# Fourteen matmuls of zeros ahead of TensorE's first inputs, in a two-layer FNet/H3 kernel

## The chip, the cores and the metric

One core of one Trainium2 chip. The metric is the device time of one execution in microseconds (us). TensorE is called PE in the profile, its weight loads PEld, VectorE DVE, ScalarE ACT, GpSimd POOL, and SyncE, which issues most loads, SP.

## The reference

Two layer kinds alternate, A B A B, each with a layer norm ahead of it and a residual around it; S = 2048 rows, D = 576 columns, f32.

```python
a = einsum("bsd,ed->bse", x, dft_hid_re); b = einsum("bsd,ed->bse", x, dft_hid_im)
A(x) = einsum("ts,bse->bte", dft_seq_re, a) - einsum("ts,bse->bte", dft_seq_im, b)
B(q, k, v): k_shift = causal conv of k with 4 taps;  kv = k_shift * v
            y = irfft(rfft(kv padded) * rfft(ssm_k padded)) + kv * ssm_D;  q * y
x = x + A(ln(x)); x = x + B(ln(x), k, v); x = x + A(ln(x)); x = x + B(ln(x), k, v)
```

## The kernel before, in words

The first A layer is turned round: the sequence transform comes first and the hidden one after it. `layer` (L300) runs steps (tb, g, k): for each block tb of 512 output rows and each of two matrices g (real and imaginary), 16 steps k multiply the normalised rows X[k] (128 rows of x) with the tile of the matrix that is loaded for that step. Every f32 operand is split into a rounded high part (ACT, `split`, L98) and the rest as a low part (DVE, L99), and a product is three matmuls: high x high, high x low, low x high. So a step is 14 matmuls of 512 columns: three into each of the accumulators s0 to s3 and two into rm. The order inside a step in the program is s0, s0, s0, s1, ..., rm, rm.

What a step needs:

- the matrix tile c: a 256 KB load by SP (L168; the first one L216), its high part by ACT (L98, `mats<-flts`), its low part by DVE (L99). Three tiles (`cs`) are kept, so the split of tile n+3 waits for the last matmul of step n.
- the row tile X[k]: a load (L683), statistics on DVE (L181 to L183), a power on POOL (L184), the bias on DVE (L190), the scaling on ACT (L191), then the high part on ACT (L195, `mats<-early`) and the low part on DVE (L197, L198). Rows from 8 on take their sums on ACT instead (L649, L651), with L650 and L652 on DVE, the power on POOL (L653), L675 on DVE and L676 on ACT.

Beside these steps runs `branch` (from L349): the convolution of k on DVE (L393 products, L398 sums, 128x1152 elements a piece) and the first stage of the long convolution, `f1_products` (L441): six matmuls of 288 or 384 columns into two of three banks bf0 to bf2, which ACT then copies out (L451) and stores (L452). It takes its data from loads of v and ssm_k (L418), split by L98 and L99 into `f1r`.

The start of the main program (L746 to L768) issues the pieces by hand: the branch's first loads, row 0, the first two c tiles, the first two groups of f1_products, row 1. Which instruction stands behind which on each engine is then settled by a scheduling layer under the kernel: it lists the instructions of each engine by its own estimate of when each could run, within the dependences that it finds and the edges that `issue_after` adds. On the chip every engine runs its list in order. All matmuls are recorded at one helper line, L75, so they are told apart here by their tiles: `s`, `rm`, `bf`, and later `bk`.

Of the kernel before, what the change touches and what calls it, by code (L numbers as in the profile page):

```python
# [10 lines left out]
F32 = mybir.dt.float32  # L11
# [4 lines left out]
P = 128  # L16
# [3 lines left out]
J = S // P  # L20
TB = 4
NT = 512
# [3 lines left out]
EPS = 1e-5  # L26
ASTAT = 8
XLEAD = 3
EARLY = 6
ROWS = (0, 1, 2, 3, 4, 5, 6, 7, 8, 9)  # L30
K_FIRST = 4
# [34 lines left out]
def fnet_h3_kernel(ctx: ExitStack, tc: tile.TileContext, x, c_mat, w_re, w_im, k_pad, v, shift_k,  # L66
                   ssm_k, ssm_d, f1c, i2c, midc, out):
    nc = tc.nc
# [5 lines left out]
    def mm(ps, lhsT, rhs, first, last, more=False):  # L74
        return nc.tensor.matmul(ps, lhsT, rhs, start=first, stop=last, skip_group_check=more).ins  # L75
# [10 lines left out]
    acc4 = [psp.tile([P, NT], F32, tag=f"s{i}", name=f"s{i}") for i in range(4)]  # L86
# [44 lines left out]
    def lay(t, at, *sizes):  # L131

        for name, words, n in sizes:
            ring.setdefault(name, Ring()).tiles.extend(t[:, at + i * words:at + (i + 1) * words] for i in range(n))
            at += n * words
        assert at <= t.shape[1], (at, t.shape, sizes)
        return at
# [9 lines left out]
    xs = mats[:, :X_END].rearrange("p (j n) -> p j n", j=J)  # L147
# [18 lines left out]
    def load_after(dst, src):  # L166
        with tc.issue_after(anchor[-1]):
            return nc.sync.dma_start(dst, src).ins  # L168
# [44 lines left out]
    def load_c(step):  # L213
        g, tb, k = step
        raw = ring["craw"]()
        anchor.append(load_after(raw, c_mat[g, tb, k]) if anchor else nc.sync.dma_start(raw, c_mat[g, tb, k]).ins)  # L216
        c = ring["cs"]()
        t = c[:, :NT], c[:, NT:]
        with behind(*stored):
            halved[:] = split(t[0], t[1], raw)  # L220
        CT[step] = t
# [3 lines left out]
    def load_w():  # L225
        lay(flts, SC_AT + CRAW * NT + 4 * D, ("wl", D, 3))
        wg = region_a(FR, "w").rearrange("p (k n) -> p k n", k=9)
        for ch in (8, *range(8)):
            w = two(wg[:, ch])
            raw = ring["wl"]()  # L230
            if ch < 8:
                nc.sync.dma_start(raw, (w_re if ch < 4 else w_im)[(ch % 4) * P:(ch % 4 + 1) * P, :])
            else:
                nc.sync.dma_start(raw[:REM], w_re[NC * P:, :])
                nc.sync.dma_start(raw[REM:], w_im[NC * P:, :])
            for lo, hi, sg in ((0, P, 1 if ch < 4 else -1),) if ch < 8 else ((0, REM, 1), (REM, P, -1)):
                if sg > 0:
                    split(w[lo:hi, 0, :], w[lo:hi, 1, :], raw[lo:hi])
                else:
                    nc.scalar.activation(w[lo:hi, 0, :], raw[lo:hi], AF.Copy, scale=-1.0)  # L240
                    nc.vector.scalar_tensor_tensor(w[lo:hi, 1, :], raw[lo:hi], -1.0,  # L241
                                                   w[lo:hi, 0, :].bitcast(F32), op0=OP.mult,
                                                   op1=OP.subtract)
            W[ch] = w
            yield
        for ch in range(9):
            load_after(w_d[ch], wg[:, ch].bitcast(F32))
            yield
# [42 lines left out]
    def finish(pending, pieces):  # L291
        while pending and pieces:
            if not isinstance(pending[0], types.GeneratorType):
                pending[0] = hidden(*pending[0])
            if next(pending[0], 0) == 0:
                pending.pop(0)
            else:
                pieces -= 1

    def layer(get_x, xres, done, pending, blocks=TB):  # L300
        steps = [(g, tb, k) for tb in range(blocks) for g in range(2) for k in range(J)]
        for n, (g, tb, k) in enumerate(steps):
# [3 lines left out]
            if n + 2 < len(steps):  # L306
                load_c(steps[n + 2])
            for i in range(XLEAD + 1 if blocks == TB else 1):
                if n + i < J:
# [346 lines left out]
    def gated(xa, q, j, junk=None, last=None):  # L656
        load_after(q, yb_d[j])
        if junk is None:
            mv, rs, _ = norm_stats(xa)
            mean, op = mv[:, 0:1], OP.subtract  # L660
        else:
            mean, rs, _ = sums(xa, junk)
            op = OP.add
        yield
        nc.vector.scalar_tensor_tensor(q, xa, mean, q, op0=op, op1=OP.mult)
        for i in range(2 if last else 1):
            cs = slice(i * HD, (i + 1) * HD) if last else slice(None)
            nc.vector.scalar_tensor_tensor(q[:, cs], q[:, cs], rs, xa[:, cs], op0=OP.mult, op1=OP.add)
            if last:
                last(i, cs)  # L670
# [9 lines left out]
    def load_x(j):  # L680
        if j < J:
            XL[j] = ring["x"]()
            nc.sync.dma_start(XL[j], x[:, j, :])  # L683
# [7 lines left out]
    def get_x0(j):  # L691
        if X[j] is None:
            if j > 0:
                load_x(j + 2)
            stats0(j)
            if j > 0:
                with behind(*stored):
                    stats0(j + 1)
            src, ln = LN[j]
            with behind(*rounded[-1:]):  # L700
                next(ln, 0)
            X[j] = to_x(src, j)
# [4 lines left out]
    def make_x1(j):  # L707
        xa, q = ring["xa"](), ring["yb"]()
        load_after(xa, xa_d[j])
        for _ in gated(xa, q, j, ring["xj"]() if j % 2 and j >= EARLY else None):  # L710
            yield
# [9 lines left out]
    def advance(j=None):  # L721
        while to_store:
            load_after(*to_store.pop(0))
        with behind(*halved, *added, *evac):
            for row in list(making):
                if next(row, 0) == 0:
                    making.remove(row)
            if j is not None:
                making.append(make_x1(j))
                next(making[-1])  # L730
# [4 lines left out]
    def done1(j, xa):  # L735
# [7 lines left out]
        if j < J - 1:  # L743
            nc.sync.dma_start(out[:, j, :], q)

    pending = []  # L746
    lay(flts, SC_AT, ("craw", NT, CRAW))
    br = branch()
    wl = load_w()
    load_x(0)  # L750
    next(br)
    get_x0(0)
    with tc.issue_after(biased[0]):
# [18 lines left out]
    for n, whole in layer(get_x0, lambda j: x[:, j, :], done0, pending):  # L772
# [40 lines left out]
        if 0 <= m and n < HOLD:  # L813
            advance(m // 2 if m % 2 == 0 and m < 2 * EARLY else None)
    T, R, t7 = {}, {}, []
# [195 lines left out]
    for n, whole in layer(get_x1, lambda j: xb_d[j], done1, pending, 1):  # L1011
# [4 lines left out]
        if n == 0:  # L1016
            for name, at in (("xa", 0), ("yb", 4 * D)):
# [3 lines left out]
                lay(gate, at, (name, D, 4))  # L1021
        advance(EARLY + ROWS.index(n) if n in ROWS else None)
        finish(pending, 1)
# [131 lines left out]
```

## Time and profile before

| | us |
|---|---|
| median of 3 runs | 1190.23 |
| lowest and highest of them | 1188.69, 1192.36 |
| the profiled execution's own time | 1191.32 |
| its span, first to last instruction | 1189.5 |
| PE busy in the span | 1168.5 (98%) |
| DVE, ACT busy | 872.8 (73%), 650.0 (55%) |

The profiled execution took 1191.32 us, of which 1.82 us lie outside the span. Times in the views are counted from the span's start. A timeline row is: start, duration, engine, line, operation, output<-input, shapes, count, and in brackets the idle time of the engine before it with what ended that. Rows of one kind that follow each other without a gap are merged, so a row "x10" holds ten instructions. PE's matmuls overlap in the records (one lasts about 0.4 us, the next starts 0.23 us behind it), so the pace of PE is read from starts, not from durations.

### The profile page before, as it was taken

The numbers are of one execution on the slowest core, as the hardware profiler recorded it, in microseconds if no ns is written. First come the engines' busy times: TensorE is split into PE (matmuls) and PEld (weight loads), VectorE is DVE, ScalarE is ACT, GpSimd is POOL, SyncE is SP. The second block draws the span as 40 slices with busy tenths as digits, with TensorE's granted clock in tenths as the row PEclk, the third lists the DMA queues.
The fourth block names the chain that finished last, engine by engine and source line by source line (L and its number), as shares of the span: only waits on it lengthen the run. The fifth ranks groups of instructions, "written<-read, shape, count | busy, mean of one in ns | idle before, by whom it ended". The sixth has DMA issues, their size and how long they took to land.

```text
span 1189.5 us, 18071 instructions
## 1 busy us (share of the span) xinstructions
PE 1168.5 (98%) x6184; PEld 987.2 (83%) x6184; DVE 872.8 (73%) x1562; ACT 650.0 (55%) x1279; POOL 75.1 (6%) x116
## 2 busy tenths in 40 slices
PE   7999999999999999999999999999999999999997
PEld 5776767888888888888888898888888888889997
DVE  7899983688777778787767665865776776775764
ACT  7865555567766668766645666534444445450200
POOL 2210000000000000001101111000000000001111
PEclk9999999999999999999999999999999999999999
DMA  9869898545656656648966777772772776795621
GB/s 340 295 197 306 269 290 267 178 139 177 225 189 198 200 160 204 186 137 239 273 197 226 235 246 231 251 250 73 255 248 71 240 273 248 266 322 158 214 83 41
DMA packets 147454, 255.65 MB, mean 215 GB/s; under 512 B 16161, under 2 KB 56353, under 8 KB 147362
## 3 DMA queue, kind: packets, MB, share of 16 engines
q1 hardware_dynamic: 111890, 210.17, 54.9%
q10 hardware_dynamic: 28560, 37.91, 9.1%
q0 software_dynamic: 6912, 6.43, 2.4%
q8 instruction: 48, 0.79, 0.3%
q14 instruction: 44, 0.36, 0.1%
HBM read 187.80 MB, written 66.65 MB: 214 GB/s over the span
## 4 chain that ended last, share of the span: by engine, by line
PE 76%; ACT 2%; DVE 2%; DMA 2%; issue 1%; POOLq 0%; ACTq 0%; DVEq 0%
PE s L75 42%; PE bk L75 29%; PE rm L75 4%; ACT flts L512 1%; ACT mid L512 1%; DMA t<-ud 1%; DVE mid L518 0%; DMA yb<-flts 0%; DMA flts<-vd 0%; DMA flts<-in_c_mat 0%; DVE flts L532 0%; DVE flts L530 0%; ACT u L98 0%; DVE flts L531 0%; DVE flts L533 0%
## 5 line engine op out<-in xcount | busy, mean ns | idle before, releaser
L75 PE MATMUL s<-mats 128*128 128x512 f32 x2088 | 543.0, 395 | 1.6 <-ACT mats L195 0.8
L75 PEld LDWEIGHTS s<-mats 128*128 128x128 f32 x2088 | 381.0, 188 | 83.2 <-issue 10.6
L99 DVE TENSOR_TENSOR mats<-flts,mats 128x512 fp32r<-128x512 f32 x206 | 141.0, 688 | 50.8 <-ACT mats L98 48.4
L98 ACT ACTIVATE mats<-flts 128x512 fp32r<-128x512 f32 x206 | 128.3, 628 | 82.6 <-PE bk L75 31.2
L75 PE MATMUL bk<-mid 128*128 128x288 f32 x704 | 127.7, 302 | 1.6 <-DVE flts L287 0.8
L75 PEld LDWEIGHTS bk<-mid 128*128 128x128 f32 x704 | 108.0, 188 | 23.7 <-ACT flts L512 5.8
L512 ACT ACTIVATE flts<-bk 128x288 f32<-128x288 f32 (+1 forms) x192 | 76.3, 406 | 90.8 <-PE bk L75 75.9
L75 PE MATMUL bk<-w,u 128*128 128x288 f32 x864 | 121.3, 296 | 1.0 <-DVE w L241 0.4
L75 PEld LDWEIGHTS bk<-w,u 128*128 128x128 f32 x864 | 117.3, 188 | 5.5 <-DVE flts L532 1.7
L518 DVE TENSOR_TENSOR mid<-flts,mid 128x576 fp32r<-128x576 f32 (+1 forms) x149 | 93.4, 629 | 18.6 <-ACT mid L512 15.2
L75 PE MATMUL rm<-mats 128*128 128x512 f32 x304 | 94.6, 391 | 0.2 <-ACT flts L512 0.2
L512 ACT ACTIVATE mid<-flts 128x576 fp32r<-128x576 f32 (+1 forms) x148 | 80.3, 575 | 11.8 <-DVE flts L533 8.5
L287 DVE TENSOR_TENSOR flts<-flts,bk 128x288 f32<-128x288 f32 x48 | 21.8, 453 | 65.8 <-PE bk L75 65.7
L451 ACT ACTIVATE flts<-bf 128x384 f32<-128x384 f32 (+1 forms) x104 | 43.2, 463 | 46.0 <-PE bf L75 45.9
L75 PE MATMUL bk<-mats 128*128 128x288 f32 (+1 forms) x376 | 67.8, 317 | 0.0
L75 PEld LDWEIGHTS rm<-mats 128*128 128x128 f32 x304 | 56.9, 188 | 12.8 <-ACT flts L512 0.6
L75 PE MATMUL s<-t,mats 128*128 128x512 f32 x264 | 65.4, 390 | 0.6 <-DVE t L99 0.3
L184 POOL TENSOR_TENSOR flts<-flts 128x1 f32<-128x1 f32 x35 | 28.7, 821 | 522.4 <-DVE flts L183 522.3
L75 PE MATMUL bk<-mats,t 128*128 128x288 f32 (+1 forms) x368 | 59.3, 303 | 0.0
L512 ACT ACTIVATE flts<-flts 64x288 f32<-64x288 f32 x128 | 56.6, 443 | 4.7
L75 PEld LDWEIGHTS s<-t,mats 128*128 128x128 f32 x264 | 49.4, 188 | 11.7 <-DVE t L99 0.8
L75 PEld LDWEIGHTS bk<-mats 128*128 128x128 f32 x376 | 55.5, 188 | 3.4
(146 smaller groups left out, 1496.7 us busy)
## 6 DMA issues: line engine op xcount, KB each, us to landing
flts<-in_c_mat SPq DMA_DIRECT2D x148, 256.0 KB, 3.3
ph<-in_c_mat SPq DMA_DIRECT2D x54, 512.0 KB, 4.5
flts<-in_c_mat SPq DMA_DIRECT2D x30, 512.0 KB, 4.8
flts<-td SPq DMA_DIRECT2D x53, 288.0 KB, 2.9
td<-flts ACTq DMA_DIRECT2D x36, 384.0 KB, 4.6
vd<-flts ACTq DMA_DIRECT2D x64, 144.0 KB, 2.7
flts<-vd SPq DMA_DIRECT2D x32, 288.0 KB, 4.1
ud<-ph ACTq DMA_DIRECT2D x12, 512.0 KB, 6.3
```

The costliest lines, as they stand in the source:

```text
L75: return nc.tensor.matmul(ps, lhsT, rhs, start=first, stop=last, skip_group_check=more).ins
L98: a = nc.scalar.activation(h, src, AF.Copy).ins
L99: return a, nc.vector.tensor_tensor(l, src, h.bitcast(F32), OP.subtract).ins
L184: pows.append(nc.gpsimd.tensor_tensor(rs, ve, mhalf, OP.pow).ins)
L287: added[:] = [nc.vector.tensor_tensor(r[:, cs], r[:, cs], ps[:, :HD], OP.add).ins]
L451: stored[:] = [nc.scalar.activation(so[:, i, :], ps[i], AF.Copy).ins]
L512: last_act.append(nc.scalar.activation(*args, **kw).ins)
L518: nc.vector.tensor_tensor(l, src, h.bitcast(F32), OP.subtract)
```

## The change

A constant and a helper are added, and the helper is called between the first row's load and the first f1_products.

```diff
+WARM = 14
...
+    def warm():
+        t = xs[:, J - 1, :NT]
+        nc.vector.memset(t.bitcast(F32), 0.0)
+        for i in range(WARM):
+            mm(acc4[3], t[:, :P], t, i == 0, i == WARM - 1)
+
     pending = []
     lay(flts, SC_AT, ("craw", NT, CRAW))
     br = branch()
     wl = load_w()
     load_x(0)
+    warm()
     next(br)
     get_x0(0)
```

`xs[:, J - 1, :NT]` is the place where row tile 15 will be written, 15 steps later; `acc4[3]` is the accumulator s3, which step 0 starts afresh. One memset on DVE is added, 128 partitions x 512, and 14 matmuls 128x128 by 128x512 on PE. No load and no store is added or taken out.

The scheduling layer sorts the lists anew, though. All orders differ only in the first part of the program: PE's last difference stands at the 471st of its 6186 matmuls, DVE's at the 216th of 1564 instructions, ACT's at the 186th, SP's at the 66th. POOL's list is the same. Line numbers of the changed kernel are higher by one here, because of the new constant (L75 is L76, L195 is L196).

At the start of PE's list, before the change, with bf the banks of f1_products and s0, s1 the first accumulators of step 0:

```order
L75 MATMUL bf1_67<-f1r_151 128x288
L75 MATMUL bf0_66<-f1r_151 128x288
L75 MATMUL s0_69<-mats_73 128x512 x2
L75 MATMUL bf0_66<-f1r_151 128x288
L75 MATMUL bf2_68<-f1r_151 128x288
...
L75 MATMUL s0_69<-mats_73 128x512
L75 MATMUL s1_70<-mats_73 128x512 x3
```

And with it:

```order
L76 MATMUL s3_72<-mats_73 128x512 x14
L76 MATMUL bf1_67<-f1r_166 128x288
L76 MATMUL bf0_66<-f1r_166 128x288
...
L76 MATMUL s0_69<-mats_73 128x512
L76 MATMUL s1_70<-mats_73 128x512
L76 MATMUL s0_69<-mats_73 128x512
L76 MATMUL s1_70<-mats_73 128x512
L76 MATMUL bf0_66<-f1r_166 128x288
L76 MATMUL bf2_68<-f1r_166 128x288
...
L76 MATMUL s0_69<-mats_73 128x512
L76 MATMUL s1_70<-mats_73 128x512
```

The zeros stand first, and two matmuls of step 0 into s1 have moved ahead of the second group of f1_products.

On ACT the same stretch, from the split of c tile 1 to the high part of row 1 (L195), before:

```order
L98 ACTIVATE mats_73<-flts_75 128x512
L451 ACTIVATE flts_75<-bf1_67 128x288
L451 ACTIVATE flts_75<-bf0_66 128x288
L98 ACTIVATE f1r_151<-flts_75 128x576
L452 DMA td_78<-flts_75 256x1x288
L451 ACTIVATE flts_75<-bf2_68 128x288
L451 ACTIVATE flts_75<-bf0_66 128x288
L98 ACTIVATE f1r_151<-flts_75 128x576
L191 ACTIVATE early_74<-early_74,flts_75 128x576
L98 ACTIVATE mats_73<-flts_75 128x512
L195 ACTIVATE mats_73<-early_74 128x576
```

And with the change:

```order
L99 ACTIVATE mats_73<-flts_75 128x512
L452 ACTIVATE flts_75<-bf0_66 128x288
L452 ACTIVATE flts_75<-bf1_67 128x288
L99 ACTIVATE f1r_166<-flts_75 128x576
L453 DMA td_78<-flts_75 256x1x288
L452 ACTIVATE flts_75<-bf2_68 128x288
L452 ACTIVATE flts_75<-bf0_66 128x288
L192 ACTIVATE early_74<-early_74,flts_75 128x576
L99 ACTIVATE f1r_166<-flts_75 128x576
L196 ACTIVATE mats_73<-early_74 128x576
L99 ACTIVATE mats_73<-flts_75 128x512
```

Bank bf0, which the second group needs back, is copied out first; the scaling and the high part of row 1 stand ahead of the split of c tile 2.

On DVE, from behind the bias of row 1 to the low part of row 1 (L198), before:

```order
L183 TENSOR_SCALAR flts_75<-flts_75 128x1
L181 BN_STATS flts_75<-early_74 128x6 x2
L99 TENSOR_TENSOR f1r_151<-flts_75,f1r_151 128x576
L182 BN_AGGR flts_75<-flts_75 128x2
L190 TENSOR_SCALAR flts_75<-flts_75 128x1
L183 TENSOR_SCALAR flts_75<-flts_75 128x1
L181 BN_STATS flts_75<-early_74 128x6 x2
L190 TENSOR_SCALAR flts_75<-flts_75 128x1
L182 BN_AGGR flts_75<-flts_75 128x2
L181 BN_STATS flts_75<-early_74 128x6
L197 TENSOR_TENSOR mats_73<-early_74,mats_73 128x64
L198 TENSOR_TENSOR mats_73<-early_74,mats_73 128x512
```

And with the change:

```order
L184 TENSOR_SCALAR flts_75<-flts_75 128x1
L182 BN_STATS flts_75<-early_74 128x6 x2
L191 TENSOR_SCALAR flts_75<-flts_75 128x1
L183 BN_AGGR flts_75<-flts_75 128x2
L182 BN_STATS flts_75<-early_74 128x6
L184 TENSOR_SCALAR flts_75<-flts_75 128x1
L182 BN_STATS flts_75<-early_74 128x6
L100 TENSOR_TENSOR f1r_166<-flts_75,f1r_166 128x576
L198 TENSOR_TENSOR mats_73<-early_74,mats_73 128x64
L199 TENSOR_TENSOR mats_73<-early_74,mats_73 128x512
```

Three instructions of later rows' statistics (one BN_STATS, one BN_AGGR, one bias) that stood ahead of row 1's low part now stand behind it.

## The prediction

> **What bounds the kernel now.** I read the page first, then the list of PE's waits, then PE's timeline of the first 19 us, then the engines that feed it. From the page, PE's line (busy time, share of the span, instructions), and from the waits the three longest (total, times, longest):
>
> ```profile
> PE 1168.5 (98%) x6184; PEld 987.2 (83%) x6184; DVE 872.8 (73%) x1562; ACT 650.0 (55%) x1279; POOL 75.1 (6%) x116
> ```
>
> ```profile
> PE bf L75 <- DVE f1r L99: 6.6, 1, 6.6
> PE bf L75 <- ACT flts L451: 1.7, 3, 1.2
> PE s L75 <- ACT mats L195: 0.8, 1, 0.8
> ```
>
> PE is busy for 98% of the span, and most of what is missing is the first wait: 6.6 us until f1_products has its operands. So PE's own pace sets the time, and what brings its work forward counts, unless a later wait eats it. PE's timeline shows that the pace is not the same everywhere:
>
> ```profile
> 6.58 1.09 PE L75 MATMUL bf<-f1r 64*128 64x288 f32 x6 [6.58 <-DVE f1r L99]
> 7.82 0.79 PE L75 MATMUL s<-mats 128*128 128x512 f32 x1
> 8.92 0.80 PE L75 MATMUL s<-mats 128*128 128x512 f32 x1 [0.30 <-DVE mats L99]
> 9.94 1.09 PE L75 MATMUL bf<-f1r 64*128 64x288 f32 x6 [0.22 <-ACT flts L451]
> 10.95 4.46 PE L75 MATMUL s<-mats 128*128 128x512 f32 x10
> 15.26 0.63 PE L75 MATMUL rm<-mats 128*128 128x512 f32 x2
> 15.73 2.90 PE L75 MATMUL s<-mats 128*128 128x512 f32 x12
> 18.47 0.61 PE L75 MATMUL rm<-mats 128*128 128x512 f32 x2
> ```
>
> Ten matmuls start between 10.95 and 15.26, 0.431 us apart; the twelve from 15.73 to 18.47 are 0.228 apart. The same form, 128x512, runs at about half pace up to 15.2 us and at full pace behind that. (The page's clock line shows full clock from the first slice on; for the start the starts of the matmuls are the evidence.) Full pace came 5.3 us after 9.94, where PE's work first runs on without a gap; the short bursts from 6.58, with gaps of 0.15, 0.30 and 0.22 us, had not brought it.
>
> **The change, part by part.** *The memset* is one more DVE instruction, behind the first of these rows of DVE's timeline:
>
> ```profile
> 0.81 0.06 DVE L174 MEMSET flts<- 128x1 f32 x1 [0.81 <-PEq L1147]
> 3.64 0.82 DVE L181 BATCH_NORM_STATS2 flts<-early 128x6 f32<-128x288 f32 x2 [2.77 <-DMA early<-in_x]
> ...
> 8.92 0.69 DVE L198 TENSOR_TENSOR mats<-early,mats 128x512 fp32r<-128x512 f32 x1
> ```
>
> A memset of 128x512 isn't in the trace. Its bounds are 0.06 us (the 128x1 memset) and 0.69 (a two-input operation of its size); I take 0.6, nearer to the row of its size. It lies in DVE's idle 2.77 us, in which DVE waits for the first row, so it costs nothing; without that cover it would cost its 0.6.
>
> *The zeros* start at about 0.87 + 0.6 = 1.5 us. At half pace fourteen take 14 x 0.431 = 6.0 us and end at 7.5; at full pace 14 x 0.228 = 3.2, ending at 4.7. PE's real work waits until 6.58, so they overrun it by 0.9 us at most. Queued behind them is the first group of f1_products, and for that waits ACT's copy L451:
>
> ```profile
> 9.19 0.69 ACT L451 ACTIVATE flts<-bf 128x288 f32<-128x288 f32 x2
> ...
> 11.67 0.68 ACT L98 ACTIVATE f1r<-flts 128x576 fp32r<-128x576 f32 x1
> 12.24 0.86 ACT L191 ACTIVATE early<-early,flts 128x576 f32<-128x576 f32 x1
> 13.03 0.63 ACT L98 ACTIVATE mats<-flts 128x512 fp32r<-128x512 f32 x1
> 13.57 0.67 ACT L195 ACTIVATE mats<-early 128x576 fp32r<-128x576 f32 x1
> ```
>
> The copies start only at 9.19, because the split of c tile 1 stands ahead of them on ACT. A first group that starts at 7.5 and takes the 1.09 of its row ends at 8.6: hidden. And the zeros' 6.0 us without a gap are longer than the 5.3 that brought full pace in the trace, so I take it that full pace is there when real work comes, or within a few matmuls.
>
> The Trainium skill, "TensorE: Matmul & The Clock Gate", section "Part 1: The HAM clock gate", puts the two paces down to a clock at half rate until a window of about 3.4 us was busy, with windows that don't start with the kernel. The trace's 0.431 against 0.228 agrees with the halving. By that rule a run of 6.0 us can just miss a whole window, since one is sure only in 6.8 us; then full pace would come later, which is the third rival.
>
> *Step 0.* The second group waits for a copy, and bf0 is now copied first: 9.19 plus half of 0.69 is about 9.6 instead of 9.94. At full pace the group takes about half of 1.09, 0.6 us. Two matmuls into s1 now stand before it, in waits that are there anyway. Ten are left, 10 x 0.228 = 2.3 us: PE is through with step 0 at 9.6 + 0.6 + 2.3 = 12.5, against 15.73. These 3.2 us are the most that the pace can give.
>
> *Step 1 is late next.* It needs row 1, whose bias (the first of these DVE rows) and low part (the last) are
>
> ```profile
> 11.82 0.21 DVE L190 TENSOR_SCALAR flts<-flts 128x1 f32<-128x1 f32 x1 [0.35 <-POOL flts L184]
> ...
> 14.46 0.21 DVE L190 TENSOR_SCALAR flts<-flts 128x1 f32<-128x1 f32 x1
> 14.59 0.20 DVE L182 BATCH_NORM_AGGREGATE flts<-flts 128x2 f32<-128x12 f32 x1
> 14.71 0.41 DVE L181 BATCH_NORM_STATS2 flts<-early 128x6 f32<-128x288 f32 x1
> 15.03 0.21 DVE L197 TENSOR_TENSOR mats<-early,mats 128x64 fp32r<-128x64 f32 x1
> 15.16 0.69 DVE L198 TENSOR_TENSOR mats<-early,mats 128x512 fp32r<-128x512 f32 x1
> ```
>
> The bias is ready at 12.03, and nothing in the change makes that earlier. In ACT's new list L191, one f1r split and L195 follow: 12.0 + 0.86 + 0.68 + 0.67, less two overlaps of 0.1, gives 14.0 for the high part (14.24 before). So PE waits 1.5 us between the steps and starts step 1 at 14.1 instead of 15.73: 1.6 us earlier, not 3.2. Half of the gain is lost here. The low part, at 15.85 before, comes some 0.6 earlier, because the three small instructions from 14.46 to 15.03 now stand behind it; PE wants it six matmuls into the step, at 14.1 + 1.4 = 15.5. If it didn't move, PE would wait 0.35 and 1.25 would be left.
>
> *From step 2 on* PE stays ahead only if ACT and DVE follow. From 10 to 30 us ACT waited for PE like this, and from 10 to 25 the engines were busy like this (PE, PEld, DVE, ACT, POOL, clock, DMA share, GB/s):
>
> ```profile
> ACT mats L98 <- PE rm L75: 1.4, 2, 0.7
> ACT flts L451 <- PE bf L75: 1.2, 2, 0.6
> ```
>
> ```profile
> 10.00:25.00 15.00, 15.00 (x62) 11.76 (x63) 13.91 (x49) 12.45 (x22) 5.66 (x9) 1.00 1.06 381
> ```
>
> ACT's waits, 2.6 us, shrink when PE is earlier, so it can follow. DVE is busy 13.91 of 15: only 1.1 us of idle time can be drawn in, and PE's next wait hangs on DVE. These are POOL's powers, DVE's row beside the long one, and PE's row:
>
> ```profile
> 41.18 0.55 POOL L653 TENSOR_TENSOR flts<-flts 128x1 f32<-128x1 f32 x1 [0.97 <-DVE flts L652]
> 49.42 4.13 POOL L653 TENSOR_TENSOR flts<-flts 128x1 f32<-128x1 f32 x1 [7.69 <-DVE flts L652]
> 55.16 0.55 POOL L653 TENSOR_TENSOR flts<-flts 128x1 f32<-128x1 f32 x1 [1.61 <-DVE flts L652]
> ```
>
> ```profile
> 49.25 2.62 DVE L393 TENSOR_TENSOR f1f<-f1f 128x1152 f32<-128x1152 f32 x2
> ```
>
> ```profile
> 56.52 1.91 PE L75 MATMUL s<-mats 128*128 128x512 f32 x6 [0.77 <-ACT mats L195]
> ```
>
> At 56.52 row 12 is late, by way of DVE, POOL, DVE and ACT. If PE comes 1.6 us earlier and DVE's chain only 1.1, the wait of 0.77 grows by 0.5 and 1.1 is left. The wait of 1.2 on L451 comes further on; this row of ACT stands just ahead of the copy:
>
> ```profile
> 95.89 0.68 ACT L98 ACTIVATE f1r<-flts 128x576 fp32r<-128x576 f32 x1 [4.76 <-DMA flts<-in_ssm_k]
> ```
>
> The split waits for a load whose slot DVE frees, so this wait, too, moves with DVE's 1.1. Behind that the lists are as before, no listed wait is longer than 0.8, and what PE has gained stays.
>
> **The sum** against the profiled execution: 1191.32 - 1.1 = 1190.2. It lay 1.1 above the median of the runs shown; on that median the same gain makes 1190.23 - 1.1 = **1189.1 us**.
>
> **The rivals**, on the median. *(1) DVE takes it all back.* If DVE's idle time can't be drawn in, because it waits there for loads (in that window the queues move 381 GB/s), the wait at 56.52 grows by 1.6 and nothing is left: 1190.2. Against it: the one wait of DVE among its rows from that window (11.82) is for POOL, not for a load.
>
> *(2) More.* The new lists could shorten the later waits too: 1.6 + 0.8 + 1.2 = 3.6 gives 1186.6. For it: the first of the two hangs on one power of 4.13 us where 0.55 is usual. Against it: the long DVE rows still stand beside it.
>
> *(3) It doesn't do what it says.* If zeros don't raise the pace, or it comes only with step 0's own run, PE is through with step 0 at about 15, and what is left is the earlier copy, some 0.3 us: 1189.9.
>
> *(4) Slower, by a pinned power.* L653 lasted 4.13 us at 49.42, while DVE ran two L393 back to back, against 0.55 at 41.18 and 55.16. The new DVE list shuffles L393 and L652 against each other between about 30 and 60 us. If a power that was free is now pinned, its row comes 3.6 us later. That decides as soon as the row had less slack than this ahead of its step, and PE's earlier start is then waited away too: 1190.2 + 3.6 = 1193.8.
>
> One more thing could take the pace back: PE's new wait of 1.5 us before step 1. At the end of the span the fall can be timed:
>
> ```profile
> 1180.00:1183.00 3.00, 1.73 (x13) 1.49 (x12) 1.13 (x4) 0.00 (x0) 0.00 (x0) 1.00 0.00 0
> 1185.00:1187.00 2.00, 0.00 (x0) 0.00 (x0) 0.26 (x1) 0.00 (x0) 0.00 (x0) 0.72 0.42 148
> ```
>
> PE stops at 1180 + 1.73, and a mean clock of 0.72 over 1185 to 1187 means half rate from 1185.9: 4.1 us of idle time. 1.5 us are far from that. The Trainium skill's rule in the same section, half rate again after an idle window of about 3.4 us, agrees with this end of the span.
>
> **How the numbers follow.** Chances: the forecast 0.56, with a range of its own from 1187.8 (1.6 kept, and 0.8 for the scatter of a median, as the three runs lie) to 1190.6; (1) 0.13; (2) 0.13; (3) 0.06; (4) 0.12. Rival (2) lies at the edge of 0.3% (3.6 us, about what a measurement of this kernel can tell from no change), so I give faster 0.10; of (4) about two thirds lie beyond it on the other side, slower 0.08; the rest, 0.82, is within. The range that should hold 8 in 10 leaves the far part of (2) and most of (4) out: 1186.6 to 1191.8.
>
> **What would show it right or wrong.** Right: fourteen matmuls into s from about 1.5 us on, in 5 to 6 us; those of step 0 0.23 apart and over by about 12.5; a wait of PE for ACT L195 of about 1.5 us and step 1 from about 14.1; ACT's waits for `rm` before 20 us gone; the later waits on L195 and L451 together no shorter than 2. Wrong: step 0 still 0.43 apart, step 1 starting before 13.5 or after 15, a power of about 4 us ahead of a wait of PE of over 2 us, or a new wait of PE between 20 and 50 us.

## The result and the profile after

| | before | with the change |
|---|---|---|
| median, us | 1190.41 (19 runs) | 1188.17 (19 runs) |
| lowest and highest, us | 1188.69, 1195.69 | 1186.96, 1189.72 |
| the profiled execution's own time, us | 1191.32 | 1188.22 |
| its span, us | 1189.5 | 1186.4 |

The ratio is 0.9977, with a 95% interval of 0.9971 to 0.9984: 2.2 us shorter, or 0.23%. That is faster, but by less than 0.3%. The forecast was 1.1 us shorter.

On the page of the changed kernel, PE's line has the fourteen matmuls more:

```profile
PE 1170.8 (99%) x6198; PEld 988.8 (83%) x6198; DVE 871.9 (73%) x1563; ACT 649.4 (55%) x1279; POOL 76.7 (6%) x116
```

PE's busy time includes 5.65 us of zeros, so it says nothing of the gain by itself. PE's longest waits (total, times, longest) are now these four:

```profile
PE s L76 <- DVE mats L749: 1.5, 1, 1.5
PE s L76 <- DVE mats L100: 1.2, 2, 1.0
PE s L76 <- ACT mats L196: 1.1, 1, 1.1
PE bf L76 <- ACT flts L452: 0.9, 2, 0.5
```

The 6.6 us at the start have become 1.5 and zeros. The wait for the high part of a row, 1.1 us, is not the one of before: that one stood at 56.52 us, this one at 14.16. PE's timeline of the first 20 us of the changed kernel:

```profile
1.49 5.65 PE L76 MATMUL s<-mats 128*128 128x512 f32 x14 [1.49 <-DVE mats L749]
7.07 0.67 PE L76 MATMUL bf<-f1r 64*128 64x288 f32 x6
7.80 0.73 PE L76 MATMUL s<-mats 128*128 128x512 f32 x2
8.71 0.73 PE L76 MATMUL s<-mats 128*128 128x512 f32 x2 [0.17 <-DVE mats L100]
9.86 0.67 PE L76 MATMUL bf<-f1r 64*128 64x288 f32 x6 [0.41 <-ACT flts L452]
10.45 2.11 PE L76 MATMUL s<-mats 128*128 128x512 f32 x8
12.40 0.61 PE L76 MATMUL rm<-mats 128*128 128x512 f32 x2
14.16 3.01 PE L76 MATMUL s<-mats 128*128 128x512 f32 x12 [1.15 <-ACT mats L196]
17.02 0.62 PE L76 MATMUL rm<-mats 128*128 128x512 f32 x2
```

The zeros run from 1.49 us, the real work comes at full pace, step 0 is through at 13.0 and step 1 starts at 14.16, 1.57 us earlier than before (15.73). The last row against its fellow of before, `rm` of step 1 at 18.47, gives a lead of 1.45 us. Matching the pairs of `rm` of the two traces in the same way, the lead is 1.45 until 50 us, 2.5 behind the place of the old wait at 56.52, 3.9 behind that of the old wait at 97.38, and 3.1 at the end. Two of the later waits of before are gone, then, and two are new, in PE's rows of the changed kernel:

```profile
120.31 0.79 PE L76 MATMUL bf<-f1r 64*128 64x384 f32 x6 [0.47 <-ACT flts L452]
1034.52 4.16 PE L76 MATMUL s<-mats,t 128*128 128x512 f32 x17 [1.01 <-DVE mats L100]
```

The second of them stands where the lists are the same before and after. In the other profiles of this study it comes and goes with lists of both kinds (1.26 us with ten zeros and the lists of before, none in experiment 4), so it is taken as scatter here; its cause was not looked for.

The two traces differ by 3.1 us and the medians by 2.2, because the profiled execution of before lay 0.9 above its median. So the question is which part of the 2.2 us the zeros bring, and which the lists that were sorted anew.

### The profile page after: what moved, and what is told of

Read it like the earlier page. It is cut to its first block, busy times and chain, and to the rows that moved or that the text cites. A ratio compares the mean times of both kernels' runs of the same rounds, so it can differ in the third digit from the quotient of the medians.

```text
span 1186.4 us, 18097 instructions
## 1 busy us (share of the span) xinstructions
PE 1170.8 (99%) x6198; PEld 988.8 (83%) x6198; DVE 871.9 (73%) x1563; ACT 649.4 (55%) x1279; POOL 76.7 (6%) x116
## 4 chain that ended last, share of the span: by engine, by line
PE 72%; DMA 3%; ACT 3%; DVE 2%; issue 1%; SPq 0%; POOLq 0%; ACTq 0%; DVEq 0%
PE s L76 40%; PE bk L76 29%; PE rm L76 4%; DMA flts<-in_c_mat 1%; ACT flts L513 1%; ACT mid L513 1%; DVE mid L519 1%; DMA vd<-flts 0%; DMA flts<-vd 0%; ACT mats L99 0%; DMA ph<-in_c_mat 0%; DMA flts<-td 0%; DMA gate<-xa 0%; DVE flts L533 0%; DVE flts L917 0%
## 5 line engine op out<-in xcount | busy, mean ns | idle before, releaser
L76 PE MATMUL s<-mats 128*128 128x512 f32 x2102 | 547.4, 395 | 3.3 <-DVE mats L749 1.5
L76 PEld LDWEIGHTS s<-mats 128*128 128x128 f32 x2102 | 383.2, 188 | 86.0 <-issue 10.8
L76 PE MATMUL bk<-mid 128*128 128x288 f32 x704 | 127.6, 302 | 1.5 <-DVE flts L288 0.7
L76 PEld LDWEIGHTS bk<-mid 128*128 128x128 f32 x704 | 108.1, 188 | 23.5 <-ACT flts L513 5.7
L76 PE MATMUL bk<-w,u 128*128 128x288 f32 x864 | 121.2, 296 | 0.9 <-DVE w L242 0.4
L76 PEld LDWEIGHTS bk<-w,u 128*128 128x128 f32 x864 | 117.3, 188 | 5.4 <-DVE flts L533 1.7
L76 PE MATMUL rm<-mats 128*128 128x512 f32 x304 | 94.4, 390 | 0.2 <-ACT flts L513 0.2
L76 PE MATMUL bk<-mats 128*128 128x288 f32 (+1 forms) x376 | 67.8, 317 | 0.0
L76 PEld LDWEIGHTS rm<-mats 128*128 128x128 f32 x304 | 56.8, 188 | 12.6 <-ACT flts L513 0.6
L76 PE MATMUL s<-t,mats 128*128 128x512 f32 x264 | 64.9, 389 | 0.0
L76 PE MATMUL bk<-mats,t 128*128 128x288 f32 (+1 forms) x368 | 59.3, 303 | 0.0
L76 PEld LDWEIGHTS bk<-mats 128*128 128x128 f32 x376 | 55.5, 188 | 3.4
L76 PEld LDWEIGHTS s<-t,mats 128*128 128x128 f32 x264 | 49.6, 188 | 10.3
```

## Experiment 1: zeros and lists apart

The lists were held by edges. At the end of the kernel's function a table names the first instructions of each engine's list, up to its last difference, and every instruction gets an edge to the one ahead of it. The edge is of the class NoSync: it settles the order in the list and makes no instruction wait for another engine. Apart from the zeros, the table is the only thing in which the kernels of experiments 1 to 3 with held lists differ. (A kernel without zeros in which the lists of before are held was not run.)

```diff
+LISTS = (
...
+)
...
+    by = {i.name: i for i in nc.cur_bb.bb.instructions}
+    for names in LISTS:
+        for a, b in zip(names, names[1:]):
+            tc.add_manual_dep(by[f"I-{b}"], f"I-{a}", mybir.DependencyInfo(
+                mybir.DependencyClass.NoSync, mybir.DependencyReason.DATA), reason="list")
```

Two kernels: the changed one with the lists of before (the zeros alone), and the one of before with the changed lists (the lists alone).

> The zeros of the change, with the four lists (PE, DVE, ACT, SP) held in the order that they had before it. Theory A, the lists matter: the pace gives its 1.1 us and no more, about 1189.3, and PE still waits for row 12 (L195) at about 55 us, 1.0 to 1.5 us, and for L451 at about 96. Theory B, the lead alone matters: the later waits go by themselves, about 1188.2 as with the change, with no wait of PE over 0.6 us between 20 and 110 us. Both: full pace by about 7 us, step 1 within 0.3 us of 14.2.

> No zeros and no memset, but the four lists held in the order that the change gives them. Theory A, the lists matter: the waits at about 56 and 97 us are gone although full pace comes only at about 15 us; about 1189.2, some 1.1 us under before. Theory B, the lead alone matters: the first steps are as before up to 0.3 us, the later waits stand, 1190.1.

Beside them two kernels with fewer zeros and nothing held. With 10 the scheduling layer keeps the lists of before, with 11 it takes those of the change.

```diff
-WARM = 14
+WARM = 10
```

```diff
-WARM = 14
+WARM = 11
```

> Ten zero matmuls instead of fourteen, with the scheduling layer left alone: it then keeps the lists of before in every row. Zeros from 1.5 to 5.8 us, a gap of 0.8 us, then the real work. If full pace comes with them: theory A 1189.3, theory B 1188.2. If 4.3 us of zeros don't bring it: 1190.3, and matmuls of step 0 0.43 us apart.

> Eleven zero matmuls, with the scheduling layer left alone: it then gives the lists of the change in every row. Zeros end at 6.2 us. Theory A: 1188.2 if full pace comes by 10 us, and about 1189.2 if it comes only with step 0, so at least 0.8 us below the run with ten zeros in either case. Theory B: the same as with ten zeros within 0.4 us.

Measured, against a median of 1190.76 of the kernel before, run beside them (35 runs; 11 of each row, 12 with ten zeros):

| zeros | lists | median, us | difference | ratio, 95% interval | step 1 starts in its profile |
|---|---|---|---|---|---|
| 14 | of before, held | 1190.37 | -0.39 | 0.9994, 0.9986 to 1.0003 | 15.15 |
| 10 | of before | 1190.98 | +0.22 | 1.0003, 0.9994 to 1.0013 | 16.59 |
| 0 | of the change, held | 1188.64 | -2.12 | 0.9981, 0.9971 to 0.9991 | 14.67 |
| 11 | of the change | 1188.73 | -2.03 | 0.9984, 0.9975 to 0.9993 | 14.87 |

The lists alone bring 2.1 us, as much as the whole change within the scatter. Zeros alone can't be told from no change: with the lists of before neither ten nor fourteen of them move the time beyond its interval, and with the changed lists eleven, fourteen and none agree within the scatter. (The profiled execution with ten zeros took 1195.52 us, the longest of its twelve; it is used here for the clock and the waits, not for its time.) So theory A has the cause right, but not its sizes: it gave 1.1 us to the zeros and 1.1 to the lists, and with fourteen zeros step 1 came at 15.15 us where both theories had 14.2. With old lists and zeros, all of the later waits are there, in PE's rows:

```profile
55.94 1.91 PE L82 MATMUL s<-mats 128*128 128x512 f32 x6 [0.77 <-ACT mats L202]
80.35 0.66 PE L82 MATMUL bf<-f1r 64*128 64x288 f32 x6 [0.29 <-ACT flts L458]
96.20 0.80 PE L82 MATMUL bf<-f1r 64*128 64x384 f32 x6 [0.57 <-ACT flts L458]
```

Part of why the zeros bring so little shows in the granted clock. These are stretches of the changed kernel, as long as one step of the clock's record, 3.41 us (PE busy, records, clock, DMA share, GB/s):

```profile
6.19:9.60 3.41, 3.02 (x14) 1.00 1.02 342
9.60:13.02 3.42, 3.16 (x16) 1.00 1.09 387
```

and these of the kernel with old lists and fourteen zeros:

```profile
6.81:10.22 3.41, 2.21 (x13) 1.00 1.01 359
10.22:13.63 3.41, 3.41 (x12) 0.50 1.07 374
```

and of ten zeros:

```profile
6.17:9.59 3.42, 1.46 (x8) 1.00 0.93 327
9.59:13.00 3.41, 2.87 (x11) 0.50 1.08 385
13.00:16.41 3.41, 3.41 (x10) 0.50 1.06 401
```

The zeros do raise the clock, at 6.2 to 7.4 us in the five profiles with zeros. But PE's first real work comes in pieces, between waits for its inputs. Behind a stretch in which PE was busy for 1.46 or 2.21 of 3.41 us the clock is half again for 3.41 or 6.82 us, just when the long run of step 0 comes; behind 3.02 and 3.16 it stayed. The kernel with eleven zeros falls back too:

```profile
7.21:10.62 3.41, 2.06 (x14) 1.00 1.05 370
10.62:14.04 3.42, 3.42 (x13) 0.50 1.02 382
```

The Trainium skill, "TensorE: Matmul & The Clock Gate", section "Part 1: The HAM clock gate", gives the fall as a matter of an idle window of about 3.4 us, and for one other kernel as a matter of frequent short idle times between groups of matmuls. The window's length agrees with these traces; they show that waits of a third of it, spread over short gaps, were enough (2.21 busy of 3.41), which is nearer to the second account.

These are single profiles. The mean clock of every execution points the same way for ten and eleven zeros, where it is 0.997 or less in 10 of 12 and 8 of 11, and for the change, where it is never so low in 19 (before: in 4 of 35). With fourteen zeros and the lists of before it is so in only 4 of 11, so the fall need not be the whole reason there.

And without zeros the clock does not come much later. With the new lists alone, PE's rows are

```profile
10.41 1.09 PE L81 MATMUL bf<-f1r 64*128 64x288 f32 x6
11.42 2.95 PE L81 MATMUL s<-mats 128*128 128x512 f32 x8
14.21 0.62 PE L81 MATMUL rm<-mats 128*128 128x512 f32 x2
14.67 2.90 PE L81 MATMUL s<-mats 128*128 128x512 f32 x12
```

Step 1 starts at 14.67 us, 0.5 behind the 14.16 with zeros, where it waits for row 1 anyway. In the nine traces of kernels without zeros the record shows full clock from 12.2 to 16.2 us on. Between the two of these that hold the changed lists at the start and lie furthest apart, step 1 starts 1.8 us apart (14.30 and 16.11): 0.5 of that is there before the clock rises, in the start of the second group of f1_products (10.12 and 10.66), and the rest comes while one of them is still at half clock. A lead read from a single trace carries this scatter.

## Experiment 2: which part of the lists

The differences fall into three stretches, cut where both lists hold the same instructions: the start (up to 30 us), the middle (31 to 64 us) and the late one (from 61 to 64 us, by engine, to 140). Kernels without zeros take the changed lists in some of them and the lists of before in the rest. Singles:

> No zeros; the changed kernel's lists only up to 30 us (7 to 16 of PE's matmuls, DVE's and ACT's instructions up to the row tiles of steps 0 to 9, three pairs of loads on SP); from there the lists of before. Theory C (each re-sorted stretch pays by itself, and what it pays is kept): step 1 starts 1.0 us earlier, as with all the new lists and no zeros, the waits at 56 and 97 us stay about 0.8 and 1.2 us long, the time is 1.0 us shorter (0.9992 of before). Theory D (a wait that stays takes back what was won ahead of it): the wait at 56 us grows to 1.5 to 1.8 us and the time is that of before within 0.3 us.

> No zeros; the changed kernel's lists only from 31 to 64 us (DVE's instructions 72 to 122, ACT's 52 to 93, PE's matmuls 203 to 245); ahead of and behind that the lists of before. Theory C: the start is that of before, the wait at 56 us is gone, that at 97 us stays, the time is 0.8 to 1.1 us shorter. Theory D: the wait at 97 us grows by what is won at 56 us, from 1.2 to about 2 us, and the time is that of before within 0.3 us.

> No zeros; the changed kernel's lists only from 61 us on (DVE from its instruction 126, ACT from 94, PE from its matmul 250, three loads on SP at 90 us); up to there the lists of before. Both theories: start and wait at 56 us as before. Theory C: the wait at 97 us is gone, a new one of 0.5 us comes at 121 us, the time is 0.6 to 1.3 us shorter, and the three stretches together make up the 2.1 us of all new lists. Theory D: only this stretch has the whole gain, 2 us.

Then pairs:

> No zeros; the changed kernel's lists up to 64 us, from there the lists of before. Theory S (the medians of the single stretches add: -0.65, +0.1, -0.3): 0.5 us shorter. Theory T (the leads seen in the traces add, and the medians of the single stretches only scatter): 1.1 us from the start and 1.0 us from the wait at 56 us, 1.5 to 2.1 us shorter, no wait at 56 us. Theory U (only all three together pay): as before within 0.5 us.

> No zeros; the lists of before up to 30 us, from there the changed kernel's. Theory S: 0.2 us shorter. Theory T: 1.0 us from the wait at 56 us and 0.5 from that at 97 us, 1.2 to 1.6 us shorter, the start as before. Theory U: as before within 0.5 us.

> No zeros; the changed kernel's lists up to 30 us and from 61 us on, between them the lists of before. Theory S: 1.0 us shorter. Theory T: 1.1 us from the start and 0.5 from the wait at 97 us, 1.3 to 1.6 us shorter, with a wait at 56 us of 0.77 us as always with the old lists there. Theory U: as before within 0.5 us.

The kernel before had medians of 1191.01 us beside the singles and 1190.88 beside the pairs (33 runs each); every other row has 11 runs. The waits are those of PE in the one profile of each, in us.

| changed lists in | median, us | difference | ratio, 95% interval | wait near 56 us | near 96 | near 121 |
|---|---|---|---|---|---|---|
| none (before) | | 0 | | 0.77 | 1.22 | none |
| start | 1190.36 | -0.65 | 0.9994, 0.9986 to 1.0003 | 0.77 | 0.65 | none |
| middle | 1191.12 | +0.11 | 1.0002, 0.9993 to 1.0010 | none | none | none |
| late | 1190.68 | -0.33 | 0.9996, 0.9988 to 1.0005 | 0.77 | none | 0.46 |
| start and middle | 1189.92 | -0.96 | 0.9992, 0.9983 to 1.0000 | none | none | none |
| middle and late | 1189.34 | -1.54 | 0.9990, 0.9981 to 0.9999 | none | none | 0.50 |
| start and late | 1189.68 | -1.20 | 0.9990, 0.9981 to 0.9999 | 0.77 | none | 0.47 |
| all three | 1188.64 | -2.12 | 0.9981, 0.9971 to 0.9991 | none | none | 0.50 |

No single stretch can be told from no change, and an interval is about 1 us to either side, so one row settles nothing. Each stretch is changed in four rows, though, and has a partner in which it isn't. The mean of those four differences is -0.79 us for the start (-0.65, -1.07, -0.87, -0.58), -0.58 for the middle (+0.11, -0.31, -1.21, -0.92) and -0.92 for the late stretch (-0.33, -0.55, -1.65, -1.16). Together 2.29, against the 2.12 of all three at once. Resampling the runs of each row gives each mean a 95% interval of some 0.5 us to either side, so each of the three can be told from zero, but not from the others. So the gain is spread over the three, as theories C and T have it. Their sizes, read from single traces, missed: C had 1.0, 0.8 to 1.1 and 0.6 to 1.3 us for the singles, against 0.65, nothing and 0.33, and T was too large for two of the three pairs. S missed by most for middle and late (0.2 us forecast, 1.54 measured). U falls, since the three pairs together average 1.2 us where it had at most 0.5. D is wrong for the start, whose share is kept past a wait that stays, and for the late stretch, which doesn't hold the whole gain.

Part of D is right, though. A smaller wait, near 80 us, isn't in the table: 0.24 us before, 0.84 with the changed start and middle, in PE's rows of these two kernels:

```profile
80.88 0.66 PE L75 MATMUL bf<-f1r 64*128 64x288 f32 x6 [0.24 <-ACT flts L451]
79.71 0.66 PE L81 MATMUL bf<-f1r 64*128 64x288 f32 x6 [0.84 <-ACT flts L457]
```

ACT waits there for a load of ssm_k (3.79 us from issue to landing before, 4.21 with start and middle). Matched by `rm`, the lead with start and middle falls from 2.33 us at 60 us to 1.18 at 84, and with the middle alone from 1.15 to 0.33; with all three stretches changed it stays at 2.1 to 2.2. Behind 97 us both have it back (2.48 and 1.62), because the wait near 96 is gone. So what a stretch wins depends on the lists behind it, and the shares are means over these cases.

The waits follow the lists without exception. The one near 56 us is there in every profile with the old middle and in none with the new; the one near 121 in every profile with the new late stretch and in none with the old. The one near 96 needs old lists in the middle and the late stretch both: it varied from 0.57 to 1.22 us over five profiles. The split on ACT ahead of it waits for a load of ssm_k, which took 5.43 us in the trace of before (issued 90.43, landed 95.86) and 3.13 in that of the change (89.11 to 92.24). Why that load is quicker was not settled; in the late lists a c tile's load stands ahead of it that before stood behind it.

## Experiment 3: the wait at 56 us

The prediction put this wait down to POOL's power of 4.13 us. One exchange on DVE takes one of the two long products from beside it. In DVE's list, before and then in the experiment:

```
L426 TENSOR_TENSOR f1f    L652 TENSOR_SCALAR flts    L393 TENSOR_TENSOR f1f    L393 TENSOR_TENSOR f1f
L426 TENSOR_TENSOR f1f    L393 TENSOR_TENSOR f1f    L652 TENSOR_SCALAR flts    L393 TENSOR_TENSOR f1f
```

> No zeros; the lists of before, but for one exchange on DVE at 49 us: one of the two products L393 stands ahead of the L652 of row 12, so that the power L653 on POOL runs beside one of them and not two. Theory P (the wait at 56 us comes from that power, which takes 4.13 us beside two products): the power takes about 1.6 us as with the new lists, L675 ends about 1.1 us earlier, the wait at 56 us is gone, the time is 0.8 us shorter. Theory Q (it comes from ACT's list, where two copies of a bank, L451, that wait for PE until 52.4 us stand ahead of row 12's scaling and high part): the power gets shorter too, but ACT is busy from 52.4 us until the high part at 55.8 us, so that the wait stays 0.6 to 0.8 us long and the time is that of before within 0.3 us.

Measured: 1190.04 us against 1191.01, ratio 0.9995 (0.9986 to 1.0004). That interval holds both forecasts, and this profile's clock happened to rise 1.3 us earlier than that of before (13.79 against 15.09), so the time doesn't decide. The rows of the profile do. The power in this kernel, POOL's row:

```profile
50.07 2.86 POOL L659 TENSOR_TENSOR flts<-flts 128x1 f32<-128x1 f32 x1 [8.96 <-DVE flts L658]
```

PE's row:

```profile
55.91 1.91 PE L81 MATMUL s<-mats 128*128 128x512 f32 x6 [0.77 <-ACT mats L201]
```

ACT's rows ahead of it:

```profile
51.78 0.71 ACT L457 ACTIVATE flts<-bf 128x288 f32<-128x288 f32 x2 [1.73 <-PE bf L81]
52.38 0.63 ACT L104 ACTIVATE mats<-flts 128x512 fp32r<-128x512 f32 x1
52.90 0.78 ACT L657 ACTIVATE early<-early,flts 128x576 f32<-128x576 f32 x1
...
53.66 0.86 ACT L682 ACTIVATE early<-early,flts 128x576 f32<-128x576 f32 x1
54.42 0.77 ACT L657 ACTIVATE early<-early,flts 128x576 f32<-128x576 f32 x1
...
55.18 0.67 ACT L201 ACTIVATE mats<-early 128x576 fp32r<-128x576 f32 x1
```

The power is 1.27 us shorter and the wait is still 0.77. That alone proves little, because the power also started 0.65 us later: it ended 0.62 us earlier (52.93 against 53.55), and PE, whose clock had risen earlier, was 0.61 us ahead here as well. Theory P's condition, L675 some 1.1 us earlier, was not reached. What decides are DVE's and ACT's rows, DVE's L675 (here L681) and ACT's L676 (here L682, above), before and then in the experiment:

```profile
53.59 0.16 DVE L675 TENSOR_TENSOR flts<-flts 128x1 f32<-128x1 f32 x1 [0.38 <-POOL flts L653]
54.28 0.86 ACT L676 ACTIVATE early<-early,flts 128x576 f32<-128x576 f32 x1
```

```profile
52.97 0.16 DVE L681 TENSOR_TENSOR flts<-flts 128x1 f32<-128x1 f32 x1 [0.38 <-POOL flts L659]
```

L675 is what the power releases, and L676 is what needs it. In both kernels it had ended 0.53 us before ACT came to L676 (53.75 and 54.28; 53.13 and 53.66), so even the power of 4.13 us was over in time. ACT stands idle for 1.73 us until PE has filled a bank, copies it out, and then works without a gap until the high part for which PE waits. The releaser is PE itself, by way of ACT's list, and theory P falls by these rows. Theory Q had the power's new length too short (1.6 forecast), and the mechanism right. No run moves ACT's two copies alone. With the changed lists the same two copies stand behind the row's scaling and high part, in ACT's rows of the changed kernel:

```profile
51.76 0.86 ACT L677 ACTIVATE early<-early,flts 128x576 f32<-128x576 f32 x1
...
53.28 0.67 ACT L196 ACTIVATE mats<-early 128x576 fp32r<-128x576 f32 x1
53.86 0.85 ACT L677 ACTIVATE early<-early,flts 128x576 f32<-128x576 f32 x1
54.62 0.39 ACT L452 ACTIVATE flts<-bf 128x288 f32<-128x288 f32 x1
```

It fits that the wait is 0.77 or 0.78 us in all seven profiles with the old middle, although the matmuls behind it start anywhere from 55.44 to 57.44 us. A wait that PE starts itself moves with PE. It costs 0.77 each time, and takes nothing back of what was gained ahead of it: with the new start alone the lead over before is 1.08 us at step 10 and 1.08 at step 12.

## Experiment 4: row 1 earlier, the try at a better version

With the zeros, step 1 waits 1.15 us for row 1, whose statistics are complete at 7.7 us while its aggregate stands behind three low parts of DVE, at 10.15. This kernel holds the changed lists, but with row 1 set forward. DVE's list from there on, with the change and then in the experiment (the row tiles in brackets):

```
L182 (1), L182 (1), L182 (2), L100 c0, L198 (0), L199 (0), L100 c1, L183 (1), L182 (2), L184 (1), L430, L183 (2), L191 (1)
L182 (1), L182 (1), L183 (1), L184 (1), L182 (2), L100 c0, L198 (0), L191 (1), L199 (0), L100 c1, L182 (2), L430, L183 (2)
```

On ACT, L192 and L196 of row 1 stand in front of a split and the second pair of copies. Behind that, row 1's low part (L198, L199) and the splits of c tile 2 move forward by four places on DVE and by one on ACT.

> With the zeros and the changed kernel's lists, and row 1 set forward: on DVE its BN_AGGR, epsilon and bias (L183, L184, L191) stand right behind its statistics instead of behind the low parts of row 0 and of two tiles (8 to 10 us), its low part in front of the statistics of row 4; on ACT its scaling and high part (L192, L196) stand in front of the second pair of bank copies. If the wait of 1.15 us ahead of step 1 is row 1's alone: step 1 starts when step 0 is through, at 12.9 to 13.2 us instead of 14.16, and the time is 1.0 us shorter than with the change, 3.2 us shorter than before. If the rest is late then (row 2, c tile 2, whose load lands at 12.9 us): the wait moves to step 2, and the time is that with the change, 2.2 us shorter than before.

Measured: 1188.57 us against 1190.88, ratio 0.9976 (0.9966 to 0.9987); 2.3 us shorter than before, against 2.2 with the change itself. PE's rows:

```profile
12.60 0.61 PE L82 MATMUL rm<-mats 128*128 128x512 f32 x2
13.05 2.88 PE L82 MATMUL s<-mats 128*128 128x512 f32 x12
15.77 0.62 PE L82 MATMUL rm<-mats 128*128 128x512 f32 x2
16.22 1.07 PE L82 MATMUL s<-mats 128*128 128x512 f32 x4
18.27 2.11 PE L82 MATMUL s<-mats 128*128 128x512 f32 x8 [0.97 <-DVE mats L205]
```

The second outcome came. Step 1 starts at 13.05, behind step 0 without a wait, but then 0.97 us go in step 2 for row 2's low part on DVE. From step 2 on PE's lead is that of the change, 1.43 us. At the start the supply of rows and tiles sets the time, and PE's pace ahead of it is worth little. No version of this study beats the change by more than the scatter.

## Why the prediction was right, and where its reasons failed

The time was forecast at 1189.1 us and is 1188.17, inside both ranges, faster but within 0.3%. The gain was twice the 1.1 us of the forecast, though. The sum holds only one term, and that term was not what brought the gain: that the time lies inside the range is in good part luck.

- **The memset and the zeros: right.** They run from 1.49 us and the first group starts behind them at 7.07, about 0.5 later than before (6.58); ACT's copy of its banks starts only at 9.41 (9.19 before), behind the split of c tile 1.
- **"Full pace is there when real work comes": right in this trace, not as a rule.** In the three traces of experiment 1 with zeros the clock fell back to half behind a stretch with waits; in that of experiment 4 it stayed. The prediction looked for the fall only in PE's wait ahead of step 1 and timed it at the end of the span, 4.1 us of idle time; shorter waits, close together, did it. It set PE's 1.5 us against those 4.1, and the falls here came without any idle time of that length.
- **Steps 0 and 1: right.** Step 0 was over at 13.0 (12.5 forecast), the wait for row 1 was 1.15 us (1.5), step 1 came at 14.16 (14.1). ACT's waits for `rm` from 10 to 30 us went from 1.4 us to 0.2.
- **What is kept of it: the failed step.** The prediction took all but some 0.3 us (the earlier copy, in rival 3) of the 1.6 us of step 1 as the gain of the zeros' pace, and let a larger wait at 56.52 take 0.5 of it, because DVE had only 1.1 us of idle time to give up. The start's lead passes 56 us whole: in the changed kernel it is still 1.4 us at 50 us and there is no wait at 56; with the new start alone, where the wait stands, it is 1.08 us on both sides. But most of the lead isn't the zeros': the same lists without zeros start step 1 at 14.67, and the zeros alone give 0.39 us less than before, not to be told from nothing. What replaces the 1.1 us is the lists' 2.1: about 0.8 from the start, 0.6 from the middle, 0.9 from the late stretch, each within some 0.5.
- **The later waits on L195 and L451, "together no shorter than 2": wrong.** Both are gone, and 0.5 us at 120 us has come; the wait of 1.0 us at 1034 us is set aside as scatter above. The cause named for the first, DVE by way of the pinned power, was the wrong one: what the power releases was ready 0.53 us before ACT came to it, and ACT's order behind PE's bank made the wait. The trace of before had the rows that show this, the two of L675 and L676 in experiment 3 and ACT's idle time ahead of the copies,

```profile
52.40 0.71 ACT L451 ACTIVATE flts<-bf 128x288 f32<-128x288 f32 x2 [1.74 <-PE bf L75]
```

  and the prediction followed the releaser only to POOL.
- **The rivals.** Rival 2, that the new lists also shorten the later waits, is what happened, in part: its 3.6 us were 3.1 in the trace and 2.2 in the medians. Its reason, a shorter power, was not the cause. Rival 3 is half true: the zeros raise the pace and yet bring nothing that these runs can tell from no change. Rival 4's event came too: a power of 4.20 us at 41.21 us in the changed kernel, beside products of DVE, but ahead of no wait of PE, so without a price.

## What to carry to other kernels

Where a scheduling layer sorts lists, adding instructions is two changes, and only holding the lists tells them apart; here the sorting was the whole gain, within a scatter of about 1 us. Before a wait is counted as a reserve that eats a lead, follow its releaser back to the end: a wait that its own engine starts, by way of another engine's list, is a fixed price, which moves along and goes away with the order that makes it. And raising a clock early pays only as far as the next supply lets the engine use it.

## What the runs showed of the hardware

The granted clock fell to half while PE was still busy for 1.46 to 2.21 of a stretch of 3.41 us, and stayed half for one or two such stretches, with PE busy for 2.87 to 3.42 us of each. In the changed kernel one stretch that was hardly fuller was not followed by a fall:

```profile
13.02:16.43 3.41, 2.27 (x10) 1.00 1.01 366
```

No run here tells where the border lies, or whether these stretches are the clock's own windows. POOL's power of 128 elements, 0.55 us by itself, took 4.13 us before, beside two products and two low parts of DVE that followed each other without a gap, 2.86 in experiment 3 beside one product and two low parts, and 1.59 in the changed kernel at 47.70, where it got in behind one product. The Trainium skill, "SBUF — State Buffer", section "Who interferes with whom", says that a DVE instruction with two inputs in SBUF and a GpSimd instruction that reads SBUF shut each other out; the traces agree, and show that a row of such instructions on DVE can keep POOL out for all of them.
